# Grouped-query attention with a gated feed-forward: scores on two row tiles, values and sums on four column tiles, in a static TensorE order

## The chip, the cores and the metric

The kernel runs on one core of one Trainium2 chip. The metric is the device time of one execution in microseconds (us). Where a kernel ran several times the median is given, with its extremes in brackets. Tiles lie in SBUF, the core's working memory, or in PSUM, where the matmuls of both kernels write. The granted clock is the share of TensorE's full speed that the profile shows as granted; "half speed" is a clock of 0.50.

## The reference, cut to what matters

```python
# q: (8, 16, 384, 64); k, v: (8, 4, 384, 64); four q heads share one k/v head
scores = q @ k.T / sqrt(64)
attn   = exp(scores - max) / (sum(exp(scores - max)) + 1e-9)
x      = (attn @ v), heads side by side          # (8, 384, 1024)

h      = relu(x @ w_in)                          # w_in 1024 x 1024
u, v   = h[..., :512], h[..., 512:]
v_n    = (v - mean(v)) / sqrt(var(v) + 1e-6)     # over the 512
v_s    = w_spatial @ v_n + b_spatial             # w_spatial 384 x 384, mixes rows
out    = (u * v_s) @ w_out                       # w_out 512 x 1024
```

Inputs and output are float32. Both kernels multiply in float16 and leave the maximum out of the softmax. Eight batches go one after the other; the feed-forward of a batch is woven into the attention of the next.

## The kernel before: the parts that matter

One head at a time. The score matmuls contract over 64 rows, so half of the 128x128 array is idle. The values' weights are 64 columns of v and 64 of ones, so that the output has the values in one half and the sums, 64 times over, in the other.

```python
for hh in range(2):                                   # two heads of a pair
    lo, hi = hh * D, hh * D + D                       # D = 64
    sc = ps_sc.tile([P, NST, 512], FP32, ...)         # one buffer
    for t in range(NST):                              # 3 blocks of 128 keys
        nc.tensor.matmul(sc[:, t, 0:S], kT2[lo:hi, t, :], qT2[lo:hi, :, :], start=True, stop=True)
    aT = att_a.tile([P, NST, S], FP16, ...)
    nc.scalar.activation(aT, sc[:, :, 0:S], AF.Exp, scale=scale)      # 128 x 1152
    for t in range(NST):
        nc.tensor.matmul(Xp[:, hh, 0:S], v1[:, t, :], aT[:, t, :],    # v1 = [v | ones]
                         start=(t == 0), stop=(t == NST - 1))
Xs = ...; nc.vector.tensor_copy(Xs, Xp[:, :, 0:S])
# later: 1/sum as exp(-ln(sum)) on ScalarE, then two multiplications on VectorE into xt
# ... cut ...
# normalisation in the feed-forward, per block st, all on VectorE, 128x1 each:
nc.vector.tensor_scalar(ve, mv[:, 1:2], eps_ln, None, op0=ALU.add)
# ... a bit trick for the first guess, then two Newton steps of four operations ...
nc.vector.tensor_scalar(v_n, v_r, mv[:, 0:1], rstd, op0=ALU.subtract, op1=ALU.mult)
# ... cut ...
# spatial mix: bias added by two matmuls with an identity, then three real ones
nc.tensor.matmul(psp[:, 0:S], ident16[:, :], bspb_hi[:, :], start=True, stop=False)
nc.tensor.matmul(psp[:, 0:S], ident16[:, :], bspb_lo[:, :], start=False, stop=False)
```

The order of TensorE's instructions is left to the scheduler of the framework.

The softmax here doesn't subtract the row's maximum and nothing guards it: scores larger than these inputs give would overflow.

Of the kernel before, what the change touches and what calls it, by code (L numbers as in the profile page):

```python
# [12 lines left out]
BF16 = mybir.dt.bfloat16  # L14
I32 = mybir.dt.int32
AF = mybir.ActivationFunctionType
ALU = mybir.AluOpType

MAGIC_RSQRT = 0x5F3759DF
# [3 lines left out]
def kernel(  # L23
# [10 lines left out]
):  # L34
    nc = tc.nc
    P = 128
# [10 lines left out]
    NPAIR_B = HQ // 2  # L47
    assert S % P == 0 and DM % P == 0 and DH % P == 0
    assert D == 64 and G % 2 == 0
    assert HQ * D == DM  # L50
# [6 lines left out]
    stage = ctx.enter_context(tc.tile_pool(name="stage", bufs=2))  # L57

    att_kv = ctx.enter_context(tc.tile_pool(name="att_kv", bufs=3))
    att_q = ctx.enter_context(tc.tile_pool(name="att_q", bufs=4))  # L60
    att_a = ctx.enter_context(tc.tile_pool(name="att_a", bufs=4))
    xt_pool = ctx.enter_context(tc.tile_pool(name="xt_pool", bufs=3))

    moe_sb = ctx.enter_context(tc.tile_pool(name="moe_sb", bufs=2))
    moe_vn = ctx.enter_context(tc.tile_pool(name="moe_vn", bufs=6))
    moe_small = ctx.enter_context(tc.tile_pool(name="moe_small", bufs=4))
    out_pool = ctx.enter_context(tc.tile_pool(name="out_pool", bufs=4))

    ps_sc = ctx.enter_context(tc.tile_pool(name="ps_sc", bufs=1, space=bass.MemoryType.PSUM))
    ps_av = ctx.enter_context(tc.tile_pool(name="ps_av", bufs=1, space=bass.MemoryType.PSUM))  # L70
    ps_moe = ctx.enter_context(tc.tile_pool(name="ps_moe", bufs=3, space=bass.MemoryType.PSUM))
    ps_misc = ps_moe
# [13 lines left out]

    ident = cst.tile([P, P], FP32, name="ident")
    make_identity(nc, ident)
    ident16 = cst.tile([P, P], FP16, name="ident16")
    nc.vector.tensor_copy(ident16, ident)  # L90

    ones_row = cst.tile([1, P], FP16, name="ones_row")
    nc.vector.memset(ones_row, 1.0)

    magic_t = cst.tile([P, NST], I32, name="magic_t")
    nc.vector.memset(magic_t, MAGIC_RSQRT)

    bsp32 = cst.tile([1, S], FP32, name="bsp32")
    nc.sync.dma_start(bsp32, moe_b_spatial.rearrange("(a s) -> a s", a=1))
    bspb_hi = cst.tile([P, S], FP16, name="bspb_hi")  # L100
    bspb_lo = cst.tile([P, S], FP16, name="bspb_lo")

# [4 lines left out]
    def mk_load_w_in(kt):  # L107
        def f():
            st_w = stage.tile([P, DFF], FP32, name=f"st_wi_{kt}", tag="st_w")
            nc.sync.dma_start(st_w, moe_w_in[kt * P : (kt + 1) * P, :])  # L110
            nc.vector.tensor_copy(w_in16[:, kt, :], st_w)
        return f

    def mk_load_w_out(m):
        def f():
            st_w = stage.tile([P, DM], FP32, name=f"st_wo_{m}", tag="st_w")
            nc.sync.dma_start(st_w, moe_w_out[m * P : (m + 1) * P, :])
            nc.vector.tensor_copy(w_out16[:, m, :], st_w)
        return f

    def mk_load_ws(st):
        def f():
            st_w = stage.tile([P, NST, S], FP32, name=f"st_ws_{st}", tag="st_ws")
            nc.sync.dma_start(st_w, moe_w_spatial.rearrange("(tt p) s -> p tt s", p=P))
            psw = ps_moe.tile([P, NST, P], FP32, name=f"psw_{st}", tag="ps_moe")
            for tt in range(NST):
                nc.tensor.transpose(psw[:, tt, :], st_w[:, tt, st * P : (st + 1) * P], ident)
            nc.scalar.copy(wsT16[:, st, :], psw)
        return f

    def mk_load_bsp():
        def f():
            bhi16 = cst.tile([1, S], FP16, name="bhi16")
            blo16 = cst.tile([1, S], FP16, name="blo16")
            lo32 = stage.tile([1, S], FP32, name="lo32", tag="lo32")
            nc.vector.tensor_copy(bhi16, bsp32)
            nc.vector.tensor_tensor(lo32, bsp32, bhi16, ALU.subtract)
            nc.vector.tensor_copy(blo16, lo32)
            bb = ps_moe.tile([P, 512], FP32, name="bb_ps", tag="ps_moe")
            nc.tensor.matmul(bb[:, 0:S], ones_row, bhi16, start=True, stop=True)  # L140
            nc.vector.tensor_copy(bspb_hi, bb[:, 0:S])
            bb2 = ps_moe.tile([P, 512], FP32, name="bb2_ps", tag="ps_moe")
            nc.tensor.matmul(bb2[:, 0:S], ones_row, blo16, start=True, stop=True)
            nc.vector.tensor_copy(bspb_lo, bb2[:, 0:S])
        return f

    init_chunks = [mk_load_bsp()]
    init_chunks += [mk_load_w_in(kt) for kt in range(NKT)]
    init_chunks += [mk_load_w_out(m) for m in range(NDT)]
    init_chunks += [mk_load_ws(st) for st in range(NST)]  # L150

    def moe_chunks_for_batch(b, xt):
        holder = {}

        def mk_u(mu):
            def f():
                if mu == 0:
                    holder["uTr"] = moe_sb.tile([P, NDT, S], FP16, name=f"uTr_{b}", tag="uTr")
                uTr = holder["uTr"]
                pu = ps_moe.tile([P, 512], FP32, name=f"pu_{b}_{mu}", tag="ps_moe")  # L160
                for kt in range(NKT):
                    nc.tensor.matmul(  # L162
                        pu[:, 0:S],
                        w_in16[:, kt, mu * P : (mu + 1) * P],
                        xt[:, kt, :],
                        start=(kt == 0),
                        stop=(kt == NKT - 1),
                    )
                nc.vector.tensor_scalar(uTr[:, mu, :], pu[:, 0:S], 0.0, None, op0=ALU.max)
            return f  # L170

        def mk_hv(st):
            def f():
                pv = ps_moe.tile([P, 512], FP32, name=f"pv_{b}_{st}", tag="ps_moe")
                for kt in range(NKT):
                    nc.tensor.matmul(  # L176
                        pv[:],
                        xt[:, kt, st * P : (st + 1) * P],
                        w_in16[:, kt, DH:DFF],
                        start=(kt == 0),  # L180
                        stop=(kt == NKT - 1),
                    )
                v_r = moe_vn.tile([P, DH], FP32, name=f"v_r_{b}_{st}", tag="v_r")
                nc.scalar.activation(v_r, pv[:], AF.Relu)
                stats = moe_small.tile([P, 6], FP32, name=f"stats_{b}_{st}", tag="stats")
                nc.vector.bn_stats(stats, v_r)
                mv = moe_small.tile([P, 8], FP32, name=f"mv_{b}_{st}", tag="mv")
                nc.vector.bn_aggr(mv[:, 0:2], stats)
                ve = mv[:, 2:3]
                y0 = mv[:, 3:4]  # L190
                tt_ = mv[:, 4:5]
                rstd = mv[:, 5:6]
                nc.vector.tensor_scalar(ve, mv[:, 1:2], eps_ln, None, op0=ALU.add)
                nc.vector.tensor_scalar(  # L194
                    y0.bitcast(I32), ve.bitcast(I32), 1, None, op0=ALU.logical_shift_right
                )
                nc.vector.tensor_tensor(y0.bitcast(I32), magic_t[:, 0:1], y0.bitcast(I32), ALU.subtract)
                for it in range(2):
                    dst = rstd if it == 1 else y0
                    nc.vector.tensor_tensor(tt_, y0, y0, ALU.mult)  # L200
                    nc.vector.tensor_tensor(tt_, tt_, ve, ALU.mult)
                    nc.vector.tensor_scalar(tt_, tt_, -0.5, 1.5, op0=ALU.mult, op1=ALU.add)  # L202
                    nc.vector.tensor_tensor(dst, y0, tt_, ALU.mult)
                v_n = moe_vn.tile([P, DH], FP16, name=f"v_n_{b}_{st}", tag="v_n")
                holder[("v_n", st)] = v_n
                nc.vector.tensor_scalar(
                    v_n, v_r, mv[:, 0:1], rstd, op0=ALU.subtract, op1=ALU.mult
                )
            return f

        def mk_sp(m):
            def f():
                if m == 0:
                    holder["gatedT"] = moe_sb.tile([P, NDT, S], FP16, name=f"gatedT_{b}", tag="gatedT")
                gatedT = holder["gatedT"]
                psp = ps_moe.tile([P, 512], FP32, name=f"psp_{b}_{m}", tag="ps_moe")
                nc.tensor.matmul(psp[:, 0:S], ident16[:, :], bspb_hi[:, :], start=True, stop=False)  # L217
# [35 lines left out]
        for st in range(NST):  # L253
            chunks.append(mk_hv(st))
# [155 lines left out]
```

## Time and profile before

| | before |
|---|---|
| median of the first 3 executions | 452.34 us (452.2 to 455.53) |
| span of the profiled execution | 451.5 us |
| busy TensorE / VectorE / ScalarE / GpSimd | 378.8 / 306.4 / 273.5 / 0.7 us |
| one batch in mid-run | 51.3 us |
| TensorE columns of one batch | 86,016, which is 36 us at the warm pace of 384 in 0.161 us |

The page of the kernel before: busy time by engine, then TensorE's busy share and its granted clock, in tenths, in 40 equal slices of the span.

```profile
PE 378.8 (84%) x1867; PEld 162.2 (36%) x1867; DVE 306.4 (68%) x892; ACT 273.5 (61%) x308; POOL 0.7 (0%) x6
...
PE   2777889799879998789879998799959898699786
...
PEclk9999999699988998999989996699997999699969
```

TensorE is the busiest but not full, and its clock falls again and again: each 6 is a slice with much half-speed time.

What it is idle for, by the view of waits (engine, tile, line, what it waited for: us in all, times, longest):

```profile
PE pu_1_2467 L162 <- DVE mv_2_2388 L194: 2.2, 1, 2.2
...
PE X_0_2256 L296 <- ACT aT_0_1_2270 L294: 1.5, 1, 1.5
...
PE X_1_2349 L296 <- ACT aT_1_1_2363 L294: 1.1, 1, 1.1
```

The first is the chain of small rsqrt operations on VectorE; the others are the exponential of the head just scored. How a wait costs twice is to be seen in the timeline (start, length, engine, line, operation, tiles, shapes, count, idle time before it and what ended that):

```profile
229.21 0.66 PE L286 MATMUL sc_1_1_2359<-qT_4_1_2347,kT_4_0_2114 64*128 64x384 f16 x3
...
231.53 0.65 PE L296 MATMUL X_1_2349<-aT_1_1_2363,v_4_0_2116 128*128 128x384 f16 x3 [1.05 <-ACT aT_1_1_2363 L294]
234.37 1.76 PE L162 MATMUL pu_1_2467<-xt_1671,w_in_113 128*128 128x384 f16 x5 [2.20 <-DVE mv_2_2388 L194]
236.06 1.14 PE L286 MATMUL sc_2_0_2442<-qT_4_2_2439,kT_4_1_2240 64*128 64x384 f16 x3
```

After waits of 1.05 and 2.20 us, five matmuls of 384 columns take 1.76 us and the three scores 1.14, against 0.66 for the same three at 229.21. The three matmuls between the two waits still ran at full speed; the clock stood at 0.50 from about 234.4 to 237.8 us.

### The profile page before, as it was taken

The page shows a single profiled execution, that of the slowest core. Times are in us where ns is not written, and L with a number is a line of the kernel's source. Part 1 is how long each engine was busy: PE and PEld are TensorE (multiplying, and loading weights), DVE is VectorE, ACT ScalarE, POOL GpSimd, SP SyncE. Part 2 cuts the span into 40 slices and gives each one's busy share as a digit, 9 for nine tenths or more (in the row PEclk, how much of TensorE's full clock was granted, in tenths as well). Part 3 has the DMA queues.
Part 4 walks back from the last instruction along what each step waited for, and adds up shares of the span by engine and source line. Part 5 has one row for each costly group of instructions (what it writes and reads, how often), then busy time and mean ns, then how long its engine had stood idle before and what let it go on. Part 6 is the DMA issues. An engine that isn't in the chain of part 4 may idle for free.

```text
span 451.5 us, 5547 instructions
## 1 busy us (share of the span) xinstructions
PE 378.8 (84%) x1867; PEld 162.2 (36%) x1867; DVE 306.4 (68%) x892; ACT 273.5 (61%) x308; POOL 0.7 (0%) x6
## 2 busy tenths in 40 slices
PE   2777889799879998789879998799959898699786
PEld 1222334344334433344324442344324443244242
DVE  5565457786596767886496766777585866866383
ACT  1555666367765677568665777367774577467711
POOL 0000000000000000000000000000000000000000
PEclk9999999699988998999989996699997999699969
DMA  6865785318302461218202460026501240002103
GB/s 184 239 190 151 229 171 133 76 27 223 93 0 63 100 198 27 51 41 233 62 0 62 126 180 20 17 51 182 135 1 44 58 162 0 1 0 94 49 0 139
DMA packets 96014, 43.03 MB, mean 95 GB/s; under 512 B 90225, under 2 KB 91378, under 8 KB 95986
## 3 DMA queue, kind: packets, MB, share of 16 engines
q1 hardware_dynamic: 95986, 42.68, 35.4%
q8 instruction: 14, 0.23, 0.2%
q14 instruction: 14, 0.11, 0.1%
HBM read 30.08 MB, written 12.58 MB: 94 GB/s over the span
## 4 chain that ended last, share of the span: by engine, by line
PE 66%; ACT 18%; DVE 12%; issue 2%; SPq 1%; DMA 1%
PE pu_1_3581 L162 1%; PE pu_1_4138 L162 1%; PE pu_1_3024 L162 1%; PE pu_1_796 L162 1%; DMA qp_0_149<-in_q_dram 1%; PE pv_0_611 L176 1%; PE pu_1_2467 L162 1%; PE pu_0_4530 L162 1%; PE pu_2_806 L162 1%; PE pu_0_2961 L162 0%; PE pu_0_1847 L162 0%; PE pu_0_1290 L162 0%; PE X_7_517 L296 0%; PE X_6_470 L296 0%; PE X_5_411 L296 0%
## 5 line engine op out<-in xcount | busy, mean ns | idle before, releaser
L162 PEld LDWEIGHTS <-w_in_113 128*128 128x128 f16 x256 | 27.4, 115 | 47.7 <-issue 41.1
L248 ACT COPY osb_0_4599<-po_0_1_4606 128x512 f32<-128x512 f32 x1 | 0.6, 586 | 11.5 <-PE po_0_1_4606 L237 11.5
L332 PE MATMUL pkt_0_124<-ident_103,kdd_0_0_122 128*128 128x128 f16 x3 | 0.5, 296 | 8.1 <-DVE ident_103 L90 8.1
L294 ACT ACTIVATE aT_0_0_165<-sc_0_0_161 128x1152 f16<-128x1152 f32 x1 | 1.1, 1131 | 9.4 <-PE sc_0_0_161 L286 9.4
L176 PE MATMUL pv_0_4445<-w_in_113,xt_3899 128*128 128x512 f16 x8 | 2.8, 410 | 3.3 <-DVE xt_3899 L311 3.3
L162 PE MATMUL pu_1_796<-xt_116,w_in_113 128*128 128x384 f16 x8 | 2.9, 516 | 2.6 <-DVE mv_1_652 L202 2.6
L162 PE MATMUL pu_1_3581<-xt_2785,w_in_113 128*128 128x384 f16 x8 | 2.9, 518 | 2.2 <-DVE mv_2_3502 L194 2.2
L162 PE MATMUL pu_1_4138<-xt_3342,w_in_113 128*128 128x384 f16 x8 | 2.9, 518 | 2.2 <-DVE mv_2_4059 L194 2.2
L162 PE MATMUL pu_1_3024<-xt_2228,w_in_113 128*128 128x384 f16 x8 | 2.9, 516 | 2.0 <-DVE mv_2_2945 L194 2.0
L162 PE MATMUL pu_1_2467<-xt_1671,w_in_113 128*128 128x384 f16 x8 | 2.7, 495 | 2.2 <-DVE mv_2_2388 L194 2.2
L176 PEld LDWEIGHTS <-xt_3899 128*128 128x128 f16 x24 | 2.1, 101 | 6.7 <-DVE xt_3899 L311 3.8
L218 PEld LDWEIGHTS <-ident_103 128*128 128x128 f16 x32 | 3.1, 97 | 3.5 <-issue 2.3
L217 PEld LDWEIGHTS <-ident_103 128*128 128x128 f16 x32 | 3.1, 98 | 1.6
L176 PEld LDWEIGHTS <-xt_116 128*128 128x128 f16 x24 | 2.4, 111 | 3.7 <-issue 2.6
L296 PEld LDWEIGHTS <-v_0_2_252 128*128 128x128 f16 x12 | 1.5, 126 | 5.9 <-issue 4.3
L176 PEld LDWEIGHTS <-xt_1671 128*128 128x128 f16 x24 | 2.2, 102 | 3.7 <-issue 2.2
L176 PEld LDWEIGHTS <-xt_2228 128*128 128x128 f16 x24 | 2.2, 102 | 3.7 <-issue 2.2
L162 PE MATMUL pu_1_1353<-xt_557,w_in_113 128*128 128x384 f16 x8 | 1.9, 359 | 2.0 <-DVE mv_2_1274 L194 2.0
L296 PEld LDWEIGHTS <-v_0_0_130 128*128 128x128 f16 x12 | 1.6, 130 | 5.2 <-issue 5.2
L176 PEld LDWEIGHTS <-xt_557 128*128 128x128 f16 x24 | 2.1, 97 | 3.4 <-issue 1.8
L162 PE MATMUL pu_1_1910<-xt_1114,w_in_113 128*128 128x384 f16 x8 | 1.6, 326 | 2.0 <-DVE mv_2_1831 L194 2.0
L237 PEld LDWEIGHTS <-gatedT_4570 128*128 128x128 f16 x24 | 2.3, 98 | 2.8 <-DVE gatedT_4570 L227 0.3
(1917 smaller groups left out, 1192.5 us busy)
## 6 DMA issues: line engine op xcount, KB each, us to landing
st_ws_499<-in_moe_w_spatial_dram SPq DMA_DIRECT2D x1, 576.0 KB, 5.2
st_ws_543<-in_moe_w_spatial_dram SPq DMA_DIRECT2D x1, 576.0 KB, 5.9
st_ws_550<-in_moe_w_spatial_dram SPq DMA_DIRECT2D x1, 576.0 KB, 3.9
st_wi_193<-in_moe_w_in_dram SPq DMA_DIRECT2D x1, 512.0 KB, 4.0
st_wi_233<-in_moe_w_in_dram SPq DMA_DIRECT2D x1, 512.0 KB, 4.8
st_wi_236<-in_moe_w_in_dram SPq DMA_DIRECT2D x1, 512.0 KB, 4.7
st_wi_292<-in_moe_w_in_dram SPq DMA_DIRECT2D x1, 512.0 KB, 4.5
st_wi_295<-in_moe_w_in_dram SPq DMA_DIRECT2D x1, 512.0 KB, 5.0
```

Source lines behind the costliest of these rows:

```text
L162: nc.tensor.matmul(pu[:, 0:S], w_in16[:, kt, mu * P : (mu + 1) * P], xt[:, kt, :], start=(kt == 0), stop=(kt == NKT - 1),)
L176: nc.tensor.matmul(pv[:], xt[:, kt, st * P : (st + 1) * P], w_in16[:, kt, DH:DFF], start=(kt == 0), stop=(kt == NKT - 1),)
L217: nc.tensor.matmul(psp[:, 0:S], ident16[:, :], bspb_hi[:, :], start=True, stop=False)
L218: nc.tensor.matmul(psp[:, 0:S], ident16[:, :], bspb_lo[:, :], start=False, stop=False)
L237: nc.tensor.matmul(po[:], gatedT[:, m, tt * P : (tt + 1) * P], w_out16[:, m, half * 512 : (half + 1) * 512], start=(m == 0), stop=(m == ND ...
L248: nc.scalar.copy(osb[:, 512:1024], po[:])
L294: nc.scalar.activation(aT, sc[:, :, 0:S], AF.Exp, scale=scale)
L296: nc.tensor.matmul(Xp[:, hh, 0:S], v1[:, t, :], aT[:, t, :], start=(t == 0), stop=(t == NST - 1),)
L332: nc.tensor.transpose(pkt[:, t, :], kdd16[:, t, :], ident16)
```

## The change

Its intent: put the idle half of the array to work. The q and k of two k/v heads lie in the two halves of the partitions, so that two 64-row tiles score two heads at once. For values and sums the array is cut into four tiles of 32 output columns, one for each of four heads; then a group of 12 matmuls (3 key blocks x 4 tiles) gives the sums of four heads, and two more such groups their values, without 64 columns of ones. Tiles of 32 columns put the features in another order, so w_in's rows are permuted when they are loaded. Beside that: exponentials of 1024 columns, casts of q, k, v moved from VectorE to GpSimd, the reciprocal square root moved to ScalarE (ln, exp), one bias matmul in place of two, and one fixed TensorE order, with feed-forward work handed out by a time budget over nine visits of each batch (a visit is one turn of the program's loop: two score units, then other work). The loads changed too: three neighbouring rows of q, k, v and w_spatial go to one partition, and k and w_spatial are read once, not twice and three times.

```diff
-        for hh in range(2): ... sc, exp, values of one head (shown above)
+    def scores(b, units):
+        for u in units:                               # two units in a visit
+            sc = ps_sc.tile([P, 2, 512], FP32, ...)   # two buffers
+            for half in range(2):
+                lo, hi = half * D, (half + 1) * D
+                nc.tensor.matmul(sc[:, half, :], kT[b][lo:hi, gp, t, :],
+                                 rhs[lo:hi, c * 512 : (c + 1) * 512], start=True, stop=True)
+            ...
+            nc.scalar.activation(aT[b, gp][:, t, :, c * 512 : (c + 1) * 512], sc, AF.Exp, scale=scale)
+
+    def values(b, gp, quad):
+        def tiles(dst, weights):
+            for t in range(NST):
+                for i in range(4):
+                    half, j = i // 2, quad * 2 + i % 2
+                    nc.tensor.matmul(dst[32 * i : 32 * (i + 1), 0:S], weights(t, half),
+                                     a[:, t, half, j * S : (j + 1) * S],
+                                     start=(t == 0), stop=(t == NST - 1))
+        tiles(sums, lambda t, half: ones32)
+        # rec = exp(-ln(sums)) on ScalarE
+        for jj in range(2):
+            tiles(X, lambda t, half: v16[:, 2 * gp + half, t, 32 * jj : 32 * (jj + 1)])
+            nc.vector.tensor_tensor(xT[b][:, gp * 4 + quad * 2 + jj, :], X[:, 0:S], rec, ALU.mult)
 ... (cut: loads, casts on GpSimd, w_in's permuted rows, bias)
-                for it in range(2): ... Newton steps on VectorE
+                nc.scalar.activation(rstd, mv[:, :, 1], AF.Ln, bias=eps_t)
+                nc.scalar.activation(rstd, rstd, AF.Exp, scale=-0.5)
 ... (cut)
+    with tc.manual_schedule(engines={PE}):            # TensorE keeps the program's order
+        ... transposes of batch 0; bias; 8 chunks of w_in; w_spatial; 4 of w_out
+        for b in range(B + 1):
+            for vi in range(VISITS if b < B else 1):  # nine visits
+                scores(b, [2 * vi, 2 * vi + 1])
+                ... values at visits 0 (of b - 1), 3, 5, 8; load_batch(b + 1) at visit 1
+                ... transposes of batch b + 1 at visits 4 to 8; of w_spatial at 3 to 5 of batch 0
+                if vi == 2 and b > 0 or b == B:
+                    queue += feed_forward(b - 1)
+                budget += per_visit
+                while queue and (b == B or done < budget):
+                    ... the next piece of the feed-forward
+                if not queue:
+                    done = max(done, budget - per_visit)
```

## The prediction

> **What bounds it now.** The page says PE busy 84%, DVE 68%, ACT 61%; no engine is full. The timeline shows a start (first exp of batch 1 at 68.4 us; PE and ACT alternate, 3.4 us per exp), seven batches of 50.6 us (first exps of batches 1 and 4: 68.4, 220.1) and a tail of about 30. Warm, TensorE streams 384 columns every 0.161 us, 512 every 0.216. A batch has 86,016 columns, 36.4 us; the other 14 are round trips (exp 1.13, reciprocal 2 x 0.84; ACT and DVE are 30% of the chain of waits), 0.11 us idle at each switch between 64-row scores and full-array matmuls, and half-speed spells after gaps: after a 2.2 us wait for the rsqrt, 384 columns take 0.32 us. The Trainium skill ("TensorE: Matmul & The Clock Gate", Part 1) says idle gaps re-throttle the array; the trace agrees.
>
> **What the change does, per batch.**
> - Scores by two concurrent row tiles: 18,432 -> 9,216 columns.
> - Values: 48 full matmuls (18,432) -> 144 column-tile matmuls, four at once: 13,824 columns of time if concurrent. Each LDWEIGHTS+MATMUL pair must then issue in 40 ns; the fastest seen are transposes, 53. The same page (Part 3) has 2.38x for three column tiles; I allow 1.55 to 2 us per group of 36.
> - Bias -1,536, k transposes -768.
> - Sum 69,900 columns, 29.5 us, plus 22 switches (2.4): 32 us.
> - ACT: 18 exps of 128x1024 (1.02, scaled from 1.13), reciprocals 8 x 0.49 instead of 16 x 0.84: 34.5 -> 24.5 us. DVE: casts go to POOL, PSUM copies and small rsqrt ops go: 38 -> 20 us. Both fall under PE.
> - The static order puts scores ahead of 2.9 us of other work per visit: exp latency is hidden, the array stays warm.
>
> **Steady state.** TensorE-bound, 32 us plus 1.5 of waits (PSUM slots held until the reciprocal; last gated block before the output matmuls): 33.5 against 50.6.
>
> **Start.** TensorE's order is fixed, and batch 0 contains transposes of batch 1 and w_spatial, whose loads come behind 6.9 MB of weights in one DMA queue with three staging buffers. DVE has the first two value multiplications before the second w_in cast, so weights stop until about 25 us. I estimate batch 1's k at 40 us, batch 0's end at 52, first feed-forward 57 (before, 66 to 68).
>
> **Sum.** 57 + seven visits of batch 1 (26) + 6 x 33.5 (201) + tail (values, 4 us left over, 18 us feed-forward, 4 us eviction and store, bubbles: 31) = 315 us.
>
> **What would show it.** Batch period 32 to 35.5 us; PE idle in mid-run under 2 us per batch, granted clock near 1.0; values at 0.16 us per four matmuls; score pairs at 0.22 us; ACT about 200 us busy in all, DVE 180; POOL 40 to 100, off the chain after the start; in the start, TensorE waiting for POOL and DMA of batch 1.
>
> **What would make it wrong.** Column tiles bound by issue (53 ns per pair: +0.4 us per group, +12 in all) or serial (+4.3 us per group, 450 in all); row tiles serial (+31); POOL casts over 2 us each, lengthening the start; PSUM slots (4) and DVE's fixed order coupling ACT waits into each visit (+1 us per visit is +60).
>
> Chances: faster by over 2% 0.96, within 2% 0.02, slower 0.02. 315 us, range 298 to 342.

## More of the kernel before

The next view has stretches of one batch: start and end, length, then busy time (and instructions) of each engine, then the mean granted clock (PEclk), the DMA share and GB/s.

```profile
120.00:171.30 51.30, 45.08 (x235) 19.79 (x234) 37.42 (x111) 34.20 (x39) 0.00 (x0) 0.93 0.33 85
171.30:222.60 51.30, 44.78 (x241) 19.75 (x239) 37.31 (x111) 35.68 (x41) 0.00 (x0) 0.97 0.34 87
222.60:273.90 51.30, 44.51 (x232) 19.22 (x231) 37.09 (x109) 33.60 (x39) 0.00 (x0) 0.93 0.33 85
```

TensorE (the first busy number) is busy for about 45 of 51.3 us, but its columns need only 36 at full pace. So each batch has two kinds of loss: some 6 us idle, and some 9 us in which it counts as busy but streams slowly (half speed, switches between tile shapes, the modelled end of each group).

## The result

| | before | after |
|---|---|---|
| median of 4 executions | 453.93 us (452.2 to 455.81) | 326.55 us (326.5 to 326.62) |
| span profiled | 451.5 us | 324.8 us |
| one batch in mid-run | 51.3 us | 34.37 us |
| busy TensorE / VectorE / ScalarE / GpSimd | 378.8 / 306.4 / 273.5 / 0.7 us | 270.4 / 161.9 / 186.2 / 39.4 us |

The ratio is 0.7193 (95% interval 0.7165 to 0.7221). Here and below a ratio is the mean time of one kernel's fast runs over the mean of the other's in the same rounds, so it is not quite the quotient of the medians quoted.

The page of the kernel after, the same lines:

```profile
PE 270.4 (83%) x2457; PEld 125.3 (39%) x2457; DVE 161.9 (50%) x316; ACT 186.2 (57%) x249; POOL 39.4 (12%) x54
...
PE   1470118799998999899989998999989998999994
...
PEclk9996558989999999999999999999999999999999
```

TensorE's share of the span is as before (83%), a warning that the share alone says little: now the loss is in the first eighth of the span (1, 1 in the busy digits), not spread over all batches. Stretches of one batch, as above:

```profile
107.97:142.34 34.37, 32.57 (x310) 1.00 0.36 115
142.34:176.71 34.37, 32.57 (x310) 1.00 0.35 116
```

(TensorE alone: busy time, clock, DMA.) TensorE is busy for 32.57 of 34.37 us at full clock. A batch has 69,888 columns, 29.3 us at the same 384 in 0.161. So of the 16.9 us that a batch lost, about 7 are columns, 5 to 6 are slow streaming (9 before, 3 now), and 4 to 5 are idle time (6.4 before, 1.8 now). The waits of one batch, and the largest of the start:

```profile
PE psw_352 L203 <- DVE ws_240 L194: 15.1, 3, 14.6
PE pk_366 L214 <- POOL k_1_281 L111: 6.8, 1, 6.8
...
PE sc_4_2034 L244 <- ACT aT_0_1954 L257: 0.9, 1, 0.9
PE sc_5_2037 L244 <- ACT aT_0_1954 L257: 0.5, 1, 0.5
...
PE psp_0_1796 L356 <- ACT rec_0_1_1755 L283: 0.2, 1, 0.2
```

The last three, and one more of 0.2, are all the waits of TensorE in a batch: 1.8 us. The timeline in mid-run:

```profile
141.97 0.39 PE L244 MATMUL sc_6_1633<-qT_0_1314,kT_1240 64*128 64x512 f16 x2
142.19 0.38 PE L244 MATMUL sc_7_1636<-qT_0_1314,kT_1240 64*128 64x512 f16 x2
142.50 0.67 PE L272 MATMUL sums_0_0_1642<-aT_0_1482,ones_103 128*32 128x384 f16 x12
143.00 0.66 PE L272 MATMUL X_0_0_0_1658<-aT_0_1482,v_3_1085 128*32 128x384 f16 x12
143.49 0.66 PE L272 MATMUL X_0_0_1_1672<-aT_0_1482,v_3_1085 128*32 128x384 f16 x12
144.08 1.47 PE L340 MATMUL pu_1_1686<-xt_1169,w_in_107 128*128 128x384 f16 x8
```

Read the starts, since the lengths hold a modelled drain. The second pair of 512-column scores starts 0.22 us after the first: two matmuls in the time of one. A group of twelve 384-column matmuls starts 0.49 to 0.50 us after the one before: four matmuls in 0.163 us, the time of one. From values back to a full-array matmul it takes 0.59, a switch of about 0.1. And the start:

```profile
24.10 0.56 DVE L288 TENSOR_TENSOR xt_307<-X_0_0_0_324,rec_0_0_321 128x384 f16<-128x384 f32 x1 [7.87 <-ACT rec_0_0_321 L284]
...
25.04 0.68 DVE L182 CAST w_in_107<-st_wi_196 128x1024 f16<-128x1024 f32 x1
25.75 1.71 SPq L181 DMA_DIRECT2D st_wi_214<-in_moe_w_in_dram  x4
...
47.23 0.83 POOL L111 CAST k_1_281<-k_1_273 128x768 f16<-128x768 f32 x1 [33.71 <-DMA k_1_273<-in_k_dram]
...
65.20 3.33 PE L303 MATMUL pv_0_627<-w_in_107,xt_307 128*128 128x512 f16 x8
```

VectorE's order has two value multiplications ahead of the cast of the second w_in chunk. The first of them waits 7.87 us for ScalarE. Until that cast is done at 25.7 us, the staging buffer that the fifth chunk needs is not free, and the load queue stands (the traffic falls to 68 GB/s in that slice, from 240 before it). Batch 1's k comes behind the weights in the queue and is cast only at 47.23 us; TensorE, whose order holds batch 1's transposes inside batch 0, waits 6.8 us for it. The larger wait comes before that: the order has w_spatial's first transposes at visit 3 of batch 0, w_spatial stands behind all of w_in in the load queue, and TensorE waits 14.6 us, until 38.98, for its cast (psw in the waits above). The first feed-forward matmul starts at 65.20. (The 9s of the clock in the first three slices are not to be trusted: at 14.97 and 15.37 us the score pairs start 0.40 apart, which is half speed.)

### The profile page after: what moved, and what is told of

It reads as the page before. It is cut to its first block, busy times and chain, and to the rows that moved or that the text cites. A ratio compares the mean times of both kernels' runs of the same rounds, so it can differ in the third digit from the quotient of the medians.

```text
span 324.8 us, 5856 instructions
## 1 busy us (share of the span) xinstructions
PE 270.4 (83%) x2457; PEld 125.3 (39%) x2457; DVE 161.9 (50%) x316; ACT 186.2 (57%) x249; POOL 39.4 (12%) x54
## 2 busy tenths in 40 slices
DMA packets 30828, 38.71 MB, mean 119 GB/s; under 512 B 1489, under 2 KB 26066, under 8 KB 30802
## 3 DMA queue, kind: packets, MB, share of 16 engines
HBM read 25.76 MB, written 12.58 MB: 118 GB/s over the span
## 4 chain that ended last, share of the span: by engine, by line
PE 65%; ACT 19%; DMA 7%; SPq 3%; DVE 2%; issue 1%; POOL 1%; DVEq 0%
DMA q_0_1_116<-in_q_dram 3%; DMA q_1_0_275<-in_q_dram 2%; ACT aT_0_262 L257 2%; SPq L181 2%; DMA ws_238<-in_moe_w_spatial_dram 2%; ACT aT_1_3573 L257 1%; ACT aT_1_2647 L257 1%; ACT aT_1_759 L257 1%; ACT aT_1_3119 L257 1%; ACT aT_1_2175 L257 1%; ACT aT_1_1703 L257 1%; ACT aT_1_1231 L257 1%; ACT aT_1_364 L257 1%; PE pv_0_627 L303 1%; ACT aT_0_545 L257 1%
## 5 line engine op out<-in xcount | busy, mean ns | idle before, releaser
L340 PEld LDWEIGHTS <-w_in_107 128*128 128x128 f16 x256 | 24.1, 98 | 18.2 <-issue 2.6
L272 PEld LDWEIGHTS <-ones_103 128*32 128x32 f16 x384 | 7.4, 97 | 15.8 <-issue 14.1
L203 PE MATMUL psw_352<-ident_102,ws_240 128*128 128x128 f16 x3 | 0.9, 287 | 15.1 <-DVE ws_240 L194 15.1
L257 ACT ACTIVATE aT_0_262<-sc_8_357 128x1024 f16<-128x1024 f32 x1 | 1.0, 1024 | 16.9 <-PE sc_8_357 L244 16.9
L257 ACT ACTIVATE aT_0_262<-sc_0_256 128x1024 f16<-128x1024 f32 x1 | 1.0, 1024 | 13.6 <-PE sc_0_256 L244 13.6
L203 PEld LDWEIGHTS <-ws_240 128*128 128x128 f16 x9 | 0.9, 117 | 15.9 <-DVE ws_240 L194 15.9
L214 PE MATMUL pk_366<-ident_102,k_1_281 128*128 128x128 f16 x6 | 0.8, 310 | 6.8 <-POOL k_1_281 L111 6.8
L257 ACT ACTIVATE aT_1_364<-sc_10_380 128x1024 f16<-128x1024 f32 x1 | 1.0, 1024 | 6.9 <-PE sc_10_380 L244 6.9
L214 PE MATMUL pk_141<-ident_102,k_0_118 128*128 128x128 f16 x6 | 0.8, 310 | 5.0 <-POOL k_0_118 L111 5.0
L244 PEld LDWEIGHTS <-kT_148 64*128 64x128 f16 x36 | 1.8, 102 | 8.3 <-issue 7.9
L111 POOL CAST k_1_281<-k_1_273 128x768 f16<-128x768 f32 x1 | 0.8, 829 | 33.7 <-DMA k_1_273<-in_k_dram 33.7
L303 PEld LDWEIGHTS <-xt_307 128*128 128x128 f16 x24 | 2.6, 113 | 4.1 <-issue 2.3
L356 PEld LDWEIGHTS <-bias_ones 128*128 128x128 f16 x32 | 3.1, 98 | 1.9 <-issue 0.7
L229 PE MATMUL pq_1_0_168<-ident_102,q_0_1_125 128*128 128x128 f16 x6 | 0.8, 307 | 3.6 <-POOL q_0_1_125 L125 3.6
L272 PEld LDWEIGHTS <-v_0_123 128*32 128x32 f16 x96 | 2.9, 109 | 2.0 <-issue 1.0
L214 PEld LDWEIGHTS <-k_1_281 128*128 128x128 f16 x6 | 0.6, 137 | 7.7 <-POOL k_1_281 L111 7.7
L379 PEld LDWEIGHTS <-gT_3919 128*128 128x128 f16 x24 | 2.3, 98 | 3.0 <-DVE gT_3919 L365 0.5
L303 PEld LDWEIGHTS <-xt_3511 128*128 128x128 f16 x24 | 2.3, 98 | 2.9 <-issue 0.3
L379 PEld LDWEIGHTS <-gT_2267 128*128 128x128 f16 x24 | 2.2, 97 | 3.0 <-DVE gT_2267 L365 0.6
L379 PEld LDWEIGHTS <-gT_2739 128*128 128x128 f16 x24 | 2.2, 97 | 3.0 <-DVE gT_2739 L365 0.6
L379 PEld LDWEIGHTS <-gT_3211 128*128 128x128 f16 x24 | 2.2, 97 | 3.0 <-DVE gT_3211 L365 0.6
```

What stands on the lines that cost most here:

```text
L111: nc.gpsimd.tensor_copy(k16, loaded[("k32", b)].rearrange("p g (t d) -> p t g d", t=NST))
L203: nc.tensor.transpose(psw[:, tt, :], ws16[:, tt, st, :], ident16)
L214: nc.tensor.transpose(pk[:, gp, t, :], k16[:, t, 2 * gp : 2 * gp + 2, :].rearrange("p g d -> p (g d)"), ident16,)
L229: nc.tensor.transpose(pq[:, jj, t, :], q16[:, t, 2 * jp + jj, :, :].rearrange("p h d -> p (h d)"), ident16,)
L244: nc.tensor.matmul(sc[:, half, :], kT[b][lo:hi, gp, t, :], rhs[lo:hi, c * 512 : (c + 1) * 512], start=True, stop=True,)
L257: nc.scalar.activation(aT[b, gp][:, t, :, c * 512 : (c + 1) * 512], sc, AF.Exp, scale=scale)
```

## The experiments

Twelve kernels. All gave the reference's result. Each changes the kernel after, but for the last, which changes the kernel before. Batch lengths are the mean distance between the starts of the batches' rstd (in e10 and e11 without the first distance, 29.2 and 30.0 us, since the scores of batch 1 were done before it).

| run | edit | median us (extremes) | ratio to before (95%) | batch us |
|---|---|---|---|---|
| after | | 326.55 (326.5 to 326.62) | 0.7193 (0.7165 to 0.7221) | 34.37 |
| e1 | scores in order tile 0, 0, 1, 1 | 342.13 (341.27 to 343.01) | 0.7534 (0.7506 to 0.7561) | 36.36 |
| e2 | values tile by tile | 327.32 (327.22 to 327.41), 2 runs | 0.7208 (0.7175 to 0.724) | 34.42 |
| e3 | TensorE order left to the scheduler | 317.52 (316.14 to 320.42) | 0.6998 (0.6946 to 0.7049) | 33.53 |
| e7 | each exp in two halves | 329.26 (329.0 to 330.34) | 0.7255 (0.7231 to 0.7279) | 34.78 |
| e9 | tile 0's values three times | 410.94 (410.28 to 411.6), 2 runs | 0.9034 (0.8999 to 0.9069) | 45.34 |
| e4 | six staging buffers | 319.01 (316.76 to 319.78) | 0.7002 (0.6966 to 0.7038) | 34.37 |
| e5 | batch 1 loaded among the weights | 309.2 (308.37 to 309.49) | 0.6794 (0.6776 to 0.6812) | 34.37 |
| e6 | feed-forward not used up early | 317.35 (315.7 to 318.9) | 0.6976 (0.6945 to 0.7006) | 32.90 |
| e8 | e5 and e6 | 299.19 (298.97 to 299.84) | 0.6599 (0.6581 to 0.6618) | 32.90 |
| e10 | e5 and e3 | 309.87 (308.64 to 311.69) | 0.6836 (0.6803 to 0.6868) | 33.53 |
| e11 | e5, e6 and e3 | 305.66 (304.37 to 305.73) | 0.673 (0.6705 to 0.6756) | 32.90 |
| e12 | before, rsqrt on ScalarE | 425.47 (424.28 to 428.22) | 0.9397 (0.9324 to 0.947) | 47.3 |

### Do the tiles run at the same time, and does their order matter?

**e1: both score matmuls of row tile 0, then both of row tile 1.**

```diff
-            for half in range(2):           # inside the loop over the two units
+        for half in range(2):
+            for gp, c, t, sc in scs:        # the two units inside
```

> The four score matmuls of a visit go row tile 0, 0, 1, 1 instead of 0, 1, 0, 1; same work, right result. If the two row tiles run concurrently and TensorE bounds the steady state, a visit takes 3 streams of 512 columns instead of 2: +0.22 us in each of 63 visits with feed-forward, about +14 us in all (341 us), batch period 34.4 -> about 36.3. Rival, that the gain came from less ACT and DVE work and the pairs are not concurrent (or PE is not the bound): within 2 us of 326.5.

Measured: 342.13 us, 15.6 more. Taken as a total it would pass for proof that the order of the row tiles costs matmul time. The trace does not bear that out. First the timeline of e1, TensorE alone:

```profile
221.30 0.61 PE L246 MATMUL sc<-qT,kT 64*128 64x512 f16 x4
221.84 0.67 PE L273 MATMUL sums<-aT,ones 128*32 128x384 f16 x12
...
248.50 0.37 PE L246 MATMUL sc<-qT,kT 64*128 64x512 f16 x1 [1.11 <-ACT aT L258]
249.41 0.71 PE L246 MATMUL sc<-qT,kT 64*128 64x512 f16 x3 [0.54 <-ACT aT L258]
250.06 6.89 PE L304 MATMUL pv<-w_in,xt 128*128 128x512 f16 x24
256.78 1.46 PE L341 MATMUL pu<-xt,w_in 128*128 128x384 f16 x8
```

The four scores take 0.54 us from start to next start, against 0.53 in the kernel after (141.97 to 142.50). So the row tiles run together in this order too. What is longer is the waits. The second unit's first matmul now stands ahead of the first unit's second, so the first exponential of a visit cannot start before both PSUM buffers are free. A batch waits 2.5 us (1.7 for exponentials, 0.4 and 0.4 for PSUM) where the kernel after waits 1.8. And then the clock falls. Stretches of one batch in e1, columns as in the kernel before:

```profile
186.43:221.68 35.25, 32.81 (x310) 15.21 (x306) 18.90 (x37) 23.25 (x32) 4.85 (x6) 1.00 0.12 46
221.68:258.56 36.88, 34.43 (x310) 15.61 (x306) 18.89 (x37) 23.24 (x32) 0.00 (x0) 0.95 0.11 44
```

In four of six whole batches the clock is 0.95 and the batch 1.7 us longer, with the same instructions and the same waits: the 24 pv matmuls after the waits then take 6.72 us instead of 5.19. So of the 15.6 us, six batches at the mean of +2.0 give some 12, and the first feed-forward matmul is 3.5 later (68.67). The number was nearly met, and its mechanism was not there. This run shows the price of a slightly longer wait, not of serial tiles.

**e2: values tile by tile** (three key blocks of tile 0, then of tile 1, and so on).

```diff
-            for t in range(NST):
-                for i in range(4):
+            for i in range(4):
+                for t in range(NST):
```

> The 12 matmuls of a value or sum tile go column tile by column tile (3 key tiles each) instead of round the four column tiles; same work, right result. If the four column tiles run concurrently only when neighbours in the queue differ, 12 matmuls take about 9 streams of 384 columns (1.45 us) instead of 3 (0.49), +2.9 us per group of 36, 32 groups: +92 us, about 418 us, period about 46. If nothing overlaps even across the change of tile: 12 streams, +4.3 us per group, about 465 us. Rival, that the LDWEIGHTS or the issue sets the pace of the column tiles anyway: within 10 us of 326.5.

Measured: 327.32 us, within 1 us of the kernel after. The expectation was missed. The timeline of e2:

```profile
143.11 0.69 PE L272 MATMUL sums<-aT,ones 128*32 128x384 f16 x12
143.61 1.17 PE L272 MATMUL X<-aT,v 128*32 128x384 f16 x24
144.71 1.47 PE L340 MATMUL pu<-xt,w_in 128*128 128x384 f16 x8
```

Twelve matmuls still take 0.50 us and the 36 take 1.60 with the switch (1.58 in the kernel after), although three in a row go to the same tile. If a matmul that waits for its own tile held up those behind it, a group of twelve would take nearly the time of three per tile in turn, 12 x 0.161 = 1.9 us. So within these groups a tile's backlog does not hold up other tiles. The kernel's careful interleaving of the four tiles is not needed.

**e9: the same three matmuls of tile 0 done three times** (the result stays right, since each repetition starts the accumulation anew).

```diff
-            for t in range(NST):
-                for i in range(4):
+            for i in (0, 0, 0, 1, 2, 3):
+                for t in range(NST):
```

> Each sum or value tile runs column tile 0's three matmuls three times over (each time cleared by start, so the result stays right): 18 matmuls instead of 12, nine of them in one column tile. After the run that ordered by column tile and lost nothing there are two readings. Concurrent tiles, each with its own queue: the group is as long as its fullest column tile, 9 streams of 384 columns (1.45 us) instead of 3 (0.49), +2.9 us per group of 36, +92 us in all, 419 us. Rival, that a 32-column matmul just takes 40 ns whatever tile it is in: 18 x 40 ns, +0.7 us per group, +23 us, 350 us.

Measured: 410.94 us. The timeline of e9:

```profile
182.46 1.64 PE L272 MATMUL sums<-aT,ones 128*32 128x384 f16 x18
183.93 3.09 PE L272 MATMUL X<-aT,v 128*32 128x384 f16 x36
186.95 0.51 PE L229 MATMUL pq<-ident,q 128*128 128x128 f16 x6
```

The total is 8 us under the 419. The 54 take 4.49 us, 2.9 more than the 36 (1.58), as expected. Serial, they would take 54 x 0.161 = 8.7; evenly spread over four tiles, 2.2; tile 0's own 27 take 27 x 0.163 = 4.4. So a group lasts as long as its fullest tile, and the other three run under it. This is direct evidence that the column tiles are concurrent. It also rules out the rival, that a 32-column matmul takes some 40 ns whatever its tile: the 54 would then take 2.2 us. In the kernel after, a weight load and its matmul pass every 41 ns (1.48 us for 36), so issue takes no longer than that.

### Is ScalarE near the limit?

**e7: each exponential of 1024 columns split in two of 512.**

```diff
-            nc.scalar.activation(aT[b, gp][:, t, :, c * 512 : (c + 1) * 512], sc, AF.Exp, scale=scale)
+            for half in range(2):
+                nc.scalar.activation(aT[b, gp][:, t, half, c * 512 : (c + 1) * 512], sc[:, half, :], AF.Exp, scale=scale)
```

> Each exp of 128x1024 is split into two of 128x512, about +0.18 us each time, +3.2 us of ACT work per batch (23.8 -> 27), right result. If TensorE bounds the steady state and ACT is off the chain but for the two scores per batch that already wait for it: +0.3 to +0.7 us per batch and about 1 to 3 us in batch 0, in all 328 to 335 us. Rival, that ACT is coupled into every visit through the order and the PSUM slots: +3 us per batch, 350 us.

Measured: 329.26 us, 2.7 more, as expected, while ScalarE is busy for 195.1 us instead of 186.2. That is 1.1 us more in a batch (24.27 instead of 23.14), not the 3.2, so the test was weaker than planned. A batch grows by 0.4 us, and its four waits by as much: the two before scores sum to 1.6 us instead of 1.4, the two for PSUM are 0.3 each instead of 0.2. About a third of ScalarE's extra time reaches the total, through these waits; the rest is hidden.

### What the static order is worth

**e3: the same program, the order of TensorE left to the scheduler.**

```diff
-    with tc.manual_schedule(engines={PE}):
+    with nullcontext():
```

> TensorE's order left to the framework's scheduler, as in the kernel before; everything else as in the changed kernel. If the static order is what hides the exp latency, TensorE waits for ACT come back in mid-run (more than 4 us per batch) and the time is 340 to 390 us. Rival, that the smaller TensorE work is the whole gain: within 2% of 326.5; in the start it may even win, since transposes that wait for late loads need not block the scores of batch 0 (first exp of batch 1 before 55 us).

Measured: 317.52 us, 9 less than the kernel after. Both expectations were missed: the fixed order is not what hides the exponentials; in this kernel it costs 9 us. The timeline of e3, at the place where the kernel after waits 0.9 and 0.5 us before sc_4 and sc_5:

```profile
130.67 0.39 PE L244 MATMUL sc<-qT,kT 64*128 64x512 f16 x2
131.00 0.60 PE L303 MATMUL pv<-w_in,xt 128*128 128x512 f16 x2
131.58 0.39 PE L244 MATMUL sc<-qT,kT 64*128 64x512 f16 x2
131.91 4.28 PE L303 MATMUL pv<-w_in,xt 128*128 128x512 f16 x19
```

The scheduler slips two pv matmuls of the next feed-forward between the scores. Only the two waits of 0.2 us are left in a batch, which takes 33.53 us (6 x 0.84 = 5 us in all), and the first feed-forward matmul starts at 62.65 (2.5 us). What is left to hide the exponentials is the order of the program, scores ahead of other work in each visit, which both have. That is argued: no run changed this order.

### Where the kernel after still loses time

**e6: do not let feed-forward time be owed.** In visits 0 and 1 of a batch the queue holds no more feed-forward than the last output piece, because the budget rule lets it catch up by one visit; then only scores and values are left, which move at ScalarE's pace.

```diff
-                    done = max(done, budget - per_visit)
+                    done = max(done, budget)
```

> One line: while the feed-forward queue is empty, its time account is kept level with the budget, so that the queue isn't made up for at once and some of it is left for visits 0 and 1 of the next batch. If the 1.4 us per batch in which the third visit's scores wait for ACT come from those two visits having nothing else to do: the wait is gone, period 34.4 -> about 33.0, the tail longer by 3 to 5 us, total 317 to 321. Rival, that ACT is late there for its own work: within 2 us of 326.5.

Measured: 317.35 us, 9.2 less, as expected. The waits of 0.9 and 0.5 us are gone and a batch takes 32.90 us. That is 1.47 less, about what the two waits were, and 8.8 in six batches. The profiled execution is the fastest of the four (315.7), and its trace shows a piece of luck: after waits of 1.46 and 0.52 us before the first pv matmuls, the same as in the kernel after, it keeps full speed (16 of them in 3.56 us; there 8 took 3.17). The longer tail that was expected (3 to 5 us) is 2.1 us: 25.1 against 23.0.

**e4: six staging buffers for weights** (SBUF for them from xt, 3 to 2, and from the feed-forward's v, 6 to 5).

```diff
-    stage = ctx.enter_context(tc.tile_pool(name="stage", bufs=3))
+    stage = ctx.enter_context(tc.tile_pool(name="stage", bufs=6))
-    xt_pool ... bufs=3, moe_v ... bufs=6
+    xt_pool ... bufs=2, moe_v ... bufs=5
```

> Six staging buffers for the weights instead of three (paid for by two xt buffers instead of three and five v buffers instead of six). If the start is long because the weight stream stops from about 17 to 25 us for want of staging buffers, and batch 1's loads stand behind it: batch 1's k cast at about 37 to 40 us instead of 47, first feed-forward at 55 to 58 instead of 65, period unchanged at 34.4, total 317 to 320 us. Rival, that the DMA rate itself (or the rate of issue) bounds the start: within 2 us of 326.5.

Measured: 319.01 us, 7.5 less, as expected. Batch 1's k is cast at 39.40 us instead of 47.23, the first feed-forward matmul starts at 57.38 instead of 65.20, and the batch is unchanged. The stop of the weight loads cost these 7.5 us.

**e5: batch 1 loaded after four chunks of w_in, w_spatial's transposes moved to batch 1, five staging buffers.**

```diff
         for kc in range(NKT):
+            if kc == 4:
+                load_batch(1)
             load_w_in(kc)
...
-                    if b == 0 and vi in (3, 4, 5):
-                        transpose_ws(vi - 3)
+                    if b == 1 and vi < 2:
+                        for st in ((0, 1), (2,))[vi]:
+                            transpose_ws(st)
```

> Batch 1's q, k, v are loaded after four of the eight w_in chunks, the w_spatial transposes moved from batch 0 to the first visits of batch 1, five staging buffers; TensorE's order still static. If the fixed order's waits for late loads are what makes the start long: scores of batch 0 run without a stop at ACT's pace, first exp of batch 1 at 36 to 40 us (59.9 now), first feed-forward at 45 to 49 (65.2), total 307 to 312. Rival, that the weights (6.9 MB plus two batches of 2.4 MB at 300 GB/s, 39 us) bound the first feed-forward anyway, further up because their casts stand behind the value multiplications in DVE's order: first feed-forward after 52, total over 314.

Measured: 309.2 us, 17.3 less, as expected. Batch 1's k is cast at 20.46 us and the first feed-forward matmul starts at 46.72. Three things change at once here. Six buffers alone gave 7.5 (e4); how the other 10 divide between the earlier load and the moved transposes is not shown. TensorE still waits 4.6 us for w_spatial's cast (until 41.87).

**e8: e5 and e6 together, static order.**

> The earlier loads of batch 1 and the evened queue together, static order. They act in different stretches (start and steady period), so the gains should add: 326.5 - 17.3 - 9.2 = 300 us, range 298 to 302; period 32.9; first feed-forward at about 47. If they overlap (the evened queue only moves waits into the start or the tail): over 304.

Measured: 299.19 us, as expected, and the best of all: first feed-forward matmul at 47.12 us, batch 32.90. The two gains add. Over the kernel before its ratio is 0.6599; divided by 0.7193 that is about 0.92 of the kernel after (in different rounds).

**e10 and e11: the same without the static order** (e10 is e5 with the edit of e3; e11 is e8 with it).

> The earlier loads with TensorE's order left to the scheduler. The scheduler's gain in steady state (34.37 -> 33.53 per batch, about 6 us) should stay and its gain in the start (about 3 us, by running scores ahead of transposes that wait for loads) should go, since those waits are gone: 303 us, range 301 to 305. If the scheduler's gain had been in the start: 308 to 309.

> All three. With the evened queue there is no wait left in mid-run that the scheduler could fill, so it should add nothing to the first of these: 299 to 301 us, period 32.9. If the scheduler finds other gaps: under 298.

Measured: 309.87 and 305.66 us. Both expectations were missed: once the start is mended, the free order gains nothing (e10 against e5, ratios 0.6836 and 0.6794 in different rounds) or loses 6.5 us (e11 against e8, in the same rounds). The timeline of e10:

```profile
48.04 0.39 PE L244 MATMUL sc<-qT,kT 64*128 64x512 f16 x2 [0.52 <-ACT aT L257]
...
56.29 0.61 PE L244 MATMUL sc<-qT,kT 64*128 64x512 f16 x2 [0.30 <-ACT aT L257]
56.83 1.14 PE L203 MATMUL psw<-ident,ws 128*128 128x128 f16 x9
57.77 2.60 PE L303 MATMUL pv<-w_in,xt 128*128 128x512 f16 x8
```

The scheduler runs all scores of batch 1 one after another at ScalarE's pace, from 42.9 to 56.3 us, and begins the feed-forward only then (57.77; e5 46.72). In mid-run it is as good as e3 (33.53 us a batch). With e6 as well both orders have 32.90. So the worth of the fixed order depends on what else is mended:

| | static | left to the scheduler |
|---|---|---|
| kernel after | 326.55 | 317.52 (e3) |
| with the start of e5 | 309.2 (e5) | 309.87 (e10) |
| with e5 and e6 | 299.19 (e8) | 305.66 (e11) |

### How much of the gain needs no tiles?

**e12: the kernel before, only the reciprocal square root moved to ScalarE.**

```diff
-                nc.vector.tensor_scalar(ve, mv[:, 1:2], eps_ln, None, op0=ALU.add)
-                ... (ten small VectorE operations in all)
+                nc.scalar.activation(y0, mv[:, 1:2], AF.Ln, bias=eps_t)
+                nc.scalar.activation(rstd, y0, AF.Exp, scale=-0.5)
```

> The kernel before with one part of the change alone: 1/sqrt(var + eps) by Ln and Exp on ACT instead of eleven small DVE operations. If a good part of what the kernel before lost per batch beside its stream was this wait (2.0 to 2.6 us per batch before the second feed-forward block) and the half-speed spell after it (384 columns at 0.32 us for some 4 us, so 2 us lost): 3 to 4.5 us less per batch over 8 batches, 418 to 430 us, period 46 to 47.5. Rival, that the round trips exp - values - copy - reciprocal set the pace and the wait only moves: over 445 us.

Measured: 425.47 us, 27.6 less than the kernel before in the same rounds (453.08), as expected. The granted clock of e12 by slices:

```profile
PEclk9999999999999999999989998999989998999979
```

The 6s of the kernel before are gone, and so is the 2.2 us wait. The scheduler's order changed with the edit, so the 27.6 us are not all shown to be that wait and its half-speed time. But about a fifth of the 127 us is to be had in the kernel before without a tile.

No run puts the tiles alone into the kernel before, or takes them alone out of the kernel after. By count they save 13,824 columns of a batch, 5.8 us at the warm pace, and e9 shows that TensorE time reaches the total: about 46 us of the 127, by this estimate. How the rest divides (less that of e12) between the larger exponentials, the second score buffer, the casts, the loads and the order is not shown.

## Why the prediction was right, and where it was not

The prediction was 315 us (298 to 342); 326.55 came. Its terms against the profiled span, worked out from first starts in the trace (65.20; 95.60 is batch 2's first exponential; six batches of 34.37; the end at 324.8):

| term | predicted | measured |
|---|---|---|
| start, to the first feed-forward matmul | 57 | 65.2 |
| rest of batch 1 | 26 | 30.4 |
| six batches | 6 x 33.5 = 201 | 206.2 |
| tail | 31 | 23.0 |
| sum | 315 | 324.8 |

- **What bounds it.** Right. TensorE is busy for 32.57 of 34.37 us of a batch at clock 1.00, and ScalarE (23.1) and VectorE (18.4) lie under it. e7 shows ScalarE's slack (1.1 us more in a batch costs 0.4) and e9 that time added to TensorE goes through: +2.9 us per value group, four groups and +11 us per batch.
- **Concurrent tiles.** Right. A score pair takes 0.22 us and four column tiles 0.163, as predicted. The doubts about issue (1.55 to 2 us for 36 matmuls) were not needed: 1.48. The Trainium skill ("TensorE: Matmul & The Clock Gate", Part 3) gives 2.38x for three column tiles; this trace shows about 3.95 for four (0.161 x 4 / 0.163), and the measurement decides. e2 and e9 went further than the prediction: each tile works off its own backlog.
- **Half-speed spells.** Right. The clock in mid-run is 1.00 where it was 0.87 to 0.97 (the three stretches shown and the next, 0.87). e1 shows by accident how near the edge this is: 0.7 us more waiting per batch brings the spells back in four batches of six. The same page (Part 1) says that idle gaps throttle the array again; the trace agrees, but at gaps of 1 to 2 us. The waits alone do not decide it: e1 keeps full speed in two batches, and e6 once where the kernel after falls to half, with the same waits.
- **Columns.** 69,900 at 29.5 us and 2.4 for 22 switches, 32 us: busy 32.57. Right.
- **Engines.** ScalarE 200 (186.2), VectorE 180 (161.9), GpSimd 40 to 100 (39.4): right, the first two 7 and 10% under, the third at the low end.
- **The static order.** This step failed. "The static order puts scores ahead of 2.9 us of other work per visit: exp latency is hidden" names the wrong cause. e3 has no fixed order and hides it better: the fixed order leaves 1.4 us of it bare in each batch and costs 9 us in this kernel. That the order of the visits hides it is argued, not shown. The fixed order is worth something (6.5 us, e8 against e11) only once e6's edit has filled visits 0 and 1.
- **Waits of a batch.** Mis-sized a little. 1.5 us were allowed for, for PSUM slots and the last gated block. 1.8 came, 1.4 of it before scores in visit 2, where the prediction had none, since it took 4 us of feed-forward to be left over; the queue holds one piece of 0.87. Together with the busy time the batch is 0.87 us longer, 5.2 us in six.
- **The start.** The largest miss. The prediction had the cause (weights stop until about 25 us for want of staging buffers; batch 1 behind them) and sized it short: k of batch 1 expected at 40, cast at 47.23; the first feed-forward at 57, begun at 65.20. It looked for TensorE waiting for batch 1 (6.8 us); the largest wait, 14.6 us, is for w_spatial. e4 and e5 confirm the cause: with more staging buffers alone it is 57.38.
- **Rest of batch 1.** 26 was sized as seven ninths of a batch; in mid-run the same stretch is 29.0 (135.38 to 164.35), and here the first pv matmuls, at half speed (8 in 3.17 us), add about 1.5.
- **Tail.** Over-sized by 8. Values and the left-over were counted on top of the last batch, but are over by its end (sums of the last group start at 300.0, six batches end at 301.8). The feed-forward of 18 us and the last store remain.

The errors are +8.2, +4.4, +5.2 and -8.0: the total was better than its terms, by luck.

## What to carry to other kernels

Where contraction or output is small, tile the array and count columns of time per tile: a group lasts as long as its fullest tile, and the order within it hardly matters, while the order of what surrounds it does. Look for the remaining loss in the start and in the places where the queue of filler work runs dry: here 27 us (326.55 to 299.19) lay there, untouched by the tiling. And when an experiment meets its number, check in the trace that the instructions it was about changed at all: e1 met its number through waits and the clock.

## What the Trainium skill lacked or had wrong

- "TensorE: Matmul & The Clock Gate", Part 3, "Measured speedup vs the span model", has 2.38x for three column tiles. In a stream of groups four column tiles ran 3.95 times as fast as one: 0.163 us for four matmuls of 384 columns, 0.161 for one. The page has no figure for a stream.
- The same part, "What overlaps and what doesn't", has weight loads overlap only where the row group differs, and matmuls as a strict FIFO. (The text above it also allows a load into the background weight buffer.) The column tiles here share their row group, and tile by tile (e2) 36 matmuls took 1.60 us with the switch, interleaved 1.58; with tile 0 filled threefold (e9), 4.49. A matmul that waits for its tile did not hold up those of other tiles. That agrees with "TensorEngine Tiling (Array Packing)", Key Properties, which has different tiles load weights and multiply in parallel.
- "TensorE: Matmul & The Clock Gate", "Back-to-back issue gap", has about 131 ns per matmul of 512 columns as the sustained rate of a stream with weight loads, and 216 as the isolated gap. Here a warm stream of 24 took 5.19 us, 216 each.
- The same page, Part 1, has the array throttled after an idle window of about 3.4 us, and beside that tells of short idle times between groups that throttle it too, without their length. Here half speed followed waits of 1.05 and 2.20 us (before), and of 1.11 and 0.54 (e1, in four batches of six); after 0.90 and 0.52 the clock stayed at 1.00. After 1.46 and 0.52 the kernel after fell to half speed and e6 did not.
- "TensorEngine Tiling (Array Packing)", Key Properties, says that a change of tiling mode drains TensorE, with no figure. Here a switch cost about 0.1 us.
- The same page says that column tiling switches Fast Weight Load off. No cost of it is to be seen here: a weight load and matmul of a column tile passed every 41 ns.
- None of the pages used here says how long SyncE is held by issuing a load: a group of four w_in loads took 5.38 us to issue at 7.17 us, while the first loads were under way, and 1.7 to 1.8 us later. Why it took longer then is not shown.
